# A linear-attention and two-layer kernel: every chunk handled in pairs of interleaved tokens

## The chip, the cores and the metric

The kernel runs on one core of a Trainium2 chip. The core has five engines that work side by side: TensorE (PE) for matrix products, VectorE (DVE), ScalarE (ACT), GpSimd (POOL) and SyncE (SP), which here only issues transfers. The metric is the time of one execution on the device in microseconds; lower is better. Inputs and outputs lie in the device's main memory, and 16 DMA engines move them.

## What is computed

The input is q, k and v for 4 batches, 8 heads, 768 tokens and 64 numbers a head, with a decay `lam` per head. Attention is linear, with a running state per head; its output, reshaped to 3072 tokens of 512 numbers, goes through two layers.

```python
for b in range(nb):                       # blocks of 64 tokens
    qb, kb, vb = q[:, :, sl], k[:, :, sl], v[:, :, sl]
    intra = einsum('bhic,bhjc->bhij', qb, kb) * Dmask       # causal, decayed
    intra = einsum('bhij,bhjd->bhid', intra, vb)
    inter = einsum('bhid,bhde->bhie', qb * lam_pow, kv_state)
    out[:, :, sl] = intra + inter
    kv_state = lam_block * kv_state + einsum('bhsd,bhse->bhde', kb * rev_pow, vb)
x = out.transpose(0, 2, 1, 3).reshape(3072, 512)
h = x @ w_in                              # 512 x 2048, "layer 1"
g = where(h >= 1, h, where(h <= -1, 0, (h + 1)**2 / 4))
y = g @ w_out                             # 2048 x 512, "layer 2"
```

The kernel doesn't follow the blocks of 64. It multiplies q by lam to the power of its position and k by lam to the inverse power, so that no decay is left in the products, and walks over chunks of 128 tokens with a plain causal mask and a state that is only added to.

## The kernel before

There are 24 chunks of 128 tokens, six to a batch of the input. Four chunks (512 tokens) make a stage of the two layers; there are six stages. Stage s of layer 1 needs `xT`, the transposed attention output, of its chunks; its 16 blocks of 128 hidden columns need the weights `w_in`, which come in four transfers (`W_IN`), each good for four blocks. A stage may be cut into parts by tokens (`PARTS`, L501; `FIRST`, L69, for stage 0): two parts make layer 1's matmuls 256 columns wide instead of 512, four parts 128, and a part can begin when its own chunks are there.

The work of a chunk, with the names that the profile shows:

- `f_load` (L533): SP issues the loads. q comes for two chunks at once, in runs of two tokens (512 bytes); k and v come one chunk and one token (256 bytes) a run, except for the first pair of chunks (`PF`, L65), which comes in runs of two tokens into `raw`. In such a pair a partition holds two neighbouring tokens, and "chunk" 2m + e of k and v holds the tokens of parity e of all 256.
- `cast` (L268) and `cast_q` (L275): multiply by the decay tables into bf16 `ks` and `qs`, on DVE for the first chunks, on POOL later. `cast_v` copies v on ACT.
- The transposes to `kT` and `qT`: on TensorE (`f_t`, `f_tq`) with copies by DVE and ACT for the first six chunks (`XT`), by transposing DMAs on SP's queue after them (`f_kx`, `f_qx`).
- `f_s` (L345): keys times queries, 16 matmuls on 64x64 tiles, into two PSUM banks (`ps`, `pt`; others early on). [...]
- `f_m` (L387): DVE multiplies them by the causal mask into `sc`, one bank at a time.
- `f_n` (L352): queries times the state `ub`, 8 matmuls on 64x64 tiles. `f_o` (L359): `sc` times v, 8 matmuls with all 128 rows and 64 columns. Both add up in `px`.
- `f_u` (L366): k times v, 8 matmuls of 128 rows by 64 columns, into the upper half of `px`; `f_sum` adds it to `state` on DVE, `f_ub` copies `state` to bf16 `ub` on ACT.
- `f_x` (L405): ACT copies `px` into `xT`.

The first pair has its own forms: 64x64 tiles in `f_op` (L395) and a separate `part` for the state's share, which DVE adds in `f_x`.

`px` is one tile of two PSUM banks. `pp_h` and `pp_y` hold two banks each for the layers; the first pair borrows some of them.

The order is not left to a scheduler. Every operation is registered by `add` with an engine, a duration, what it needs and a due time; `run_plan` (L202) plays this through on a small model of the engines and transfers, and issues each engine's instructions in the order that comes out, earliest due first among those ready. Each engine then works strictly in that order. `l_seq` (L509) fixes the order of the layers' pieces; `L0` (L73) that of stage 0 as (part, weight) pairs. `o_due` (L524) puts a chunk's last operation `LEAD` ahead of the layer 1 piece that needs it. `ORDER`, `GATE` and `W_AFTER` fix how the loads and the eight weight transfers on POOL's queue follow each other: a gated transfer waits until an earlier one has landed. In the later chunks (`MERGED`) the s of the next chunk and n, o, u of this one stand together as one operation of TensorE, so that its tiling mode changes less often; in the others s with n and o with u stand apart, with layer work between.

## Time and profile before

| What | Value |
|---|---|
| Median of 8 runs | 218.8 us (218.39 to 219.65) |
| The profiled execution | 218.96 us |
| Its span, first to last instruction | 217.1 us |
| First matmul of layer 1 | 18.68 us |
| Last matmul ends | 214.24 us |
| TensorE busy | 200.1 us |
| VectorE, ScalarE, GpSimd busy | 143.6, 115.5, 60.9 us |
| Packets of DMA under 512 bytes | 65810 of 87465 |

The page of the profile lists busy times, forty slices of the span, the chain of work that ended last, and the costliest groups of instructions. The timeline shows instructions in order of time: start, duration, engine, line, what is written from what, how often, and in brackets how long the engine had been idle before and who released it. [...] The profiled execution was about as long as the median run.

### The profile page before, as it was taken

To read this page: it belongs to the slowest core of one execution; us is meant where nothing else is said; L and a number is where in the kernel's file an instruction comes from. 1 tells how busy PE (TensorE), PEld (TensorE's weight loads), DVE (VectorE), ACT (ScalarE), POOL (GpSimd) and SP (SyncE) were. 2 spreads that over 40 slices of the span, in tenths; PEclk is the share of its full clock that TensorE was granted. 3 is DMA by queue.
4 is the path that set the end of the run, shared out by engine and by line. 5 is a ranking of instruction groups with operands and counts; after the bars stand their busy time and mean duration, and the time that the engine had idled before them with its cause. 6 is when DMAs were issued, how large, how long until landed. Compare 5 with 4: busy or idle time off the path is not lost.

```text
span 217.1 us, 5115 instructions
## 1 busy us (share of the span) xinstructions
PE 200.1 (92%) x2122; PEld 125.2 (58%) x2147; DVE 143.6 (66%) x233; ACT 115.5 (53%) x199; POOL 60.9 (28%) x67
## 2 busy tenths in 40 slices
PE   0579799999999999889999999999999999999994
PEld 0356687675647855657767666654444444444443
DVE  3394786889743992797899996857876364554301
ACT  3454677364617664676565846746645544455030
POOL 5590094065633413833506325100000000000000
PEclk9999999999999999999999999999999999999999
DMA  5999999999998999999999999991101001110122
GB/s 165 278 215 206 249 179 219 226 213 213 172 203 182 223 168 221 175 231 209 235 186 204 174 282 179 271 284 39 48 3 48 23 25 48 51 48 0 48 100 97
DMA packets 87465, 34.42 MB, mean 159 GB/s; under 512 B 65810, under 2 KB 84498, under 8 KB 87442
## 3 DMA queue, kind: packets, MB, share of 16 engines
q1 hardware_dynamic: 83216, 29.89, 66.8%
q0 software_dynamic: 4224, 4.19, 11.7%
q8 instruction: 17, 0.28, 0.6%
q14 instruction: 6, 0.05, 0.1%
q10 hardware_dynamic: 2, 0.00, 0.0%
HBM read 27.26 MB, written 6.29 MB: 155 GB/s over the span
## 4 chain that ended last, share of the span: by engine, by line
PE 53%; issue 1%; DVE 0%
PE py L474 24%; PE ph L426 23%; PE px L363 2%; PE ps L349 2%; PE py L468 1%; PE px L370 1%; PE px L356 1%; PE ph L468 0%; PE pt L349 0%; DVE osb L486 0%
## 5 line engine op out<-in xcount | busy, mean ns | idle before, releaser
L426 PE MATMUL ph<-xT,w_in_sb 128*128 128x256 bf16 (+2 forms) x764 | 95.8, 274 | 3.4 <-ACT xT L415 2.6
L435 ACT ACTIVATE r<-ph,one 128x512 bf16<-128x512 f32 x96 | 65.6, 688 | 48.4 <-PE ph L426 36.9
L474 PE MATMUL py<-w_out_sb,gT 128*128 128x512 bf16 x347 | 85.6, 379 | 1.8 <-issue 1.1
L426 PEld LDWEIGHTS <-w_in_sb 128*128 128x128 bf16 x768 | 64.1, 98 | 28.0 <-issue 3.6
L474 PEld LDWEIGHTS <-gT 128*128 128x128 bf16 x368 | 34.7, 98 | 36.9
L445 DVE TENSOR_SCALAR t<-r 128x1024 bf16<-128x1024 bf16 x48 | 25.6, 533 | 22.3 <-ACT r L435 22.3
L456 DVE TENSOR_TENSOR gT<-w,t 128x1024 bf16<-128x1024 bf16 x48 | 39.1, 815 | 1.5
L451 DVE TENSOR_TENSOR w<-r,t 128x1024 bf16<-128x1024 bf16 x48 | 36.2, 753 | 1.4
L281 POOL TENSOR_TENSOR qs<-x0f,tab_q 128x512 bf16<-128x512 f32 x23 | 27.2, 1202 | 26.5 <-DMA x0f<-in_q_dram 19.4
L273 POOL TENSOR_TENSOR ks<-x1f,tab_k 128x512 bf16<-128x512 f32 x20 | 23.6, 1188 | 35.8 <-issue 15.6
L479 ACT COPY osb<-py 128x512 f32<-128x512 f32 x23 | 13.4, 585 | 22.3 <-PE py L474 21.2
L393 DVE TENSOR_TENSOR sc<-ps,causal 128x512 bf16<-128x512 f32 x22 | 15.1, 687 | 13.4 <-PE pt L349 13.1
L415 ACT CAST xT<-px 128x512 bf16<-128x512 f32 x22 | 12.9, 585 | 13.6 <-PE px L370 8.3
L393 DVE TENSOR_TENSOR sc<-pt,causal 128x512 bf16<-128x512 f32 x21 | 14.3, 681 | 0.0
L295 ACT CAST v<-x2f 128x512 bf16<-128x512 f32 x22 | 13.6, 618 | 0.2 <-DMA x2f<-in_v_dram 0.2
L377 DVE TENSOR_TENSOR state<-state,px 128x256 f32<-128x256 f32 x16 | 6.7, 419 | 8.2 <-ACT xT L415 4.7
L349 PEld LDWEIGHTS <-kT 64*64 64x64 bf16 x384 | 6.6, 112 | 6.9 <-issue 4.6
L385 ACT CAST ub<-state 128x256 bf16<-128x256 f32 x20 | 8.0, 402 | 4.6 <-DVE state L375 2.5
L349 PE MATMUL ps<-qT,kT 64*64 64x128 bf16 x184 | 10.0, 230 | 0.5 <-DVE kT L314 0.5
L363 PE MATMUL px<-sc,v 128*64 128x128 bf16 x176 | 9.1, 225 | 0.0
L349 PE MATMUL pt<-qT,kT 64*64 64x128 bf16 x168 | 8.7, 222 | 0.0
L363 PEld LDWEIGHTS <-v 128*64 128x64 bf16 x176 | 5.6, 109 | 4.3 <-issue 2.5
(62 smaller groups left out, 77.9 us busy)
## 6 DMA issues: line engine op xcount, KB each, us to landing
x0f<-in_q_dram SPq DMA_DIRECT2D x12, 512.0 KB, 5.5
out_dram<-osb SPq DMA_DIRECT2D x23, 256.0 KB, 2.6
x1f<-in_k_dram SPq DMA_DIRECT2D x22, 256.0 KB, 5.1
x2f<-in_v_dram SPq DMA_DIRECT2D x22, 256.0 KB, 5.4
w_in_sb<-in_moe_w_in_dram POOLq DMA_DIRECT2D x4, 512.0 KB, 8.2
w_out_sb<-in_moe_w_out_dram POOLq DMA_DIRECT2D x4, 512.0 KB, 8.0
raw<-in_k_dram SPq DMA_DIRECT2D x1, 512.0 KB, 5.5
raw<-in_v_dram SPq DMA_DIRECT2D x1, 512.0 KB, 6.7
```

The source lines that it names most:

```text
L273: eng.tensor_tensor(ho(ks[c]), hs(qkv_ld[c, 1]), ho(_bc(tab, 2, D)), op=AX.mult)
L281: eng.tensor_tensor(ho(qs[m, e]), hs(qkv_ld[m, 0][:, :, e]), ho(_bc(tab_q[:, e, m % (NCB // 2), :], 2, D)), op=AX.mult)
L295: nc.scalar.copy(out=v_sb[c % NV], in_=qkv_ld[c, 2])
L349: nc.tensor.matmul(pst[c, r][HD[i], b, :], lhsT=kT[c][HD[r], b, HD[i]], rhs=q_cols(2 * (c // 2) + i if c // 2 in PF else c, b, HD[r]), sta ...
L363: nc.tensor.matmul(px[HD[g], j, :128], lhsT=v_sb[c % NV][:, 2 * j + g, :], rhs=sc_sb[c][:, r, b, :], start=(c % NCB == 0 and j % 2 == 0), ...
L393: nc.vector.tensor_tensor(sc_sb[c][:, g], pst[c, g], _bc(causal, 1, HP), op=AX.mult)
L426: nc.tensor.matmul(ph[:, j * m:(j + 1) * m], lhsT=w_in_sb[:, ko, (ni + j) * 128:(ni + j + 1) * 128], rhs=xT[s][:, ko, tok], start=(ko == 0 ...
L435: nc.scalar.activation(out=o, in_=x, func=AF.Relu, bias=one[:, 0:1])
L445: nc.vector.tensor_scalar(t, r, 0.5, 1.0, op0=AX.mult, op1=AX.min)
L451: nc.vector.tensor_tensor(w, r, t, op=AX.subtract)
L456: nc.vector.tensor_tensor(gT[s][:, f - RW * n:f, tok].rearrange("p (a b) m -> p a b m", a=RW), w.rearrange("p a (b m) -> p a b m", m=m), t ...
L474: nc.tensor.matmul(py_t[s, ms], lhsT=gT[s][:, ko, ms * 128:(ms + 1) * 128], rhs=w_out_sb[:, ko, :], start=(ko == 0), stop=(ko == FO - 1))
```

## The change

All chunks now go through the paired form; the single-chunk form is gone.

- k and v are loaded for two chunks at a time in runs of two tokens, like q. The keys, queries, state and output products of a pair are three operations of TensorE: A (`f_n` first phase, `f_s` of parity 0), B (`f_s` of parity 1 with `f_n`'s second phase inside), C (`f_c`, both parities, both chunks). `f_c` and `f_u` run on 64x64 tiles: 32 matmuls each for a pair.
- `px` has two banks, one for each chunk of the pair, and `f_n` works in two phases, so that the two row halves of the array write to different banks at a time. `f_u` writes to banks of its own instead of `px`. A third pair of a batch computes only the state of its first chunk.
- For the first pair the state's product is `f_n0`, with a state `ubz` padded with zeros.
- `warm` issues matmuls with no use for the result, in the gaps that the plan shows on TensorE before its own time 18000 ns: as many as fill 0.8 of each gap at 107 ns.
- Some early casts are split between DVE and POOL (`SHARED`), kT of chunk 1 is copied by ACT, x of chunk 1 too.
- The orders and due times differ: stage 0 takes all four weights for its first part and then for the second; stage 1 has two parts instead of four, stage 3 one instead of two; `LEAD` is 6000 instead of 4500; the loads' gates are new. From pair 5 on (`MERGED`) u of the next pair stands behind C.

```diff
-    LD = 6
+    LD = 3
...
     RW, NR = 2, 3
-    XT, NQT, NQK, RING = 6, 4, 4, 3
+    XT = 6
+    NQT, NQK, RING = 4, 4, 3
     W_IN = (4, 4, 4, 4)
-    MERGED = tuple(range(12, 24))
-    LATE = (3,)
+    MERGED = tuple(range(5,12))
     SWITCH = 96
     W_OF = [i for i, n in enumerate(W_IN) for _ in range(n)]
-    ORDER = [0, 1, 2, 3, (0, 0), (0, 1), (0, 2), (0, 3), 4, (1, 0), (1, 1), 5, (1, 2), (1, 3)]
-    PF = (0,)
-    D0 = (8350, 11900, 15450, 19000)
+    ORDER = [0, 1, (0, 0), (0, 1), (0, 2), (0, 3), 2, (1, 0), (1, 1), 3, (1, 2), (1, 3)]
+    D0 = (8350, 10000, 15450, 17000)
     FIRST = [(0, 2), (2, 4)]
-    L0 = [(0, 0), (0, 1), (1, 0), (1, 1), (0, 2), (1, 2), (0, 3), (1, 3)]
-    GATE = {(0, 0): ("lq", 1), 4: 1, 6: 5}
-    LORD = {0: (0, 1, 2), 2: (0, 1, 2)}
+    L0 = [(0, 0), (0, 1), (0, 2), (0, 3), (1, 0), (1, 1), (1, 2), (1, 3)]
+    GATE = {(0, 0): ('lq', 1), 2: 0, (1, 0): 2, 3: 4, (1, 2): 4}
...
-    px = pp_o.tile([128, HP, 256], F32)
+    px = pp_o.tile([128, 2, HP, 128], F32)
...
     MMS, FETCH = {"s": 16, "u": 8}, 1300
-    FIRST_BYTE = 2350
-    LDD, QXD, KXD, STD = 20000, 7000, 7000, 3000
-    ON_POOL, ON_DVE = (1,), ((0, 1),)
-    W_AFTER = {1: ("cq", 1, 1)}
+    FIRST_BYTE = 2750
+    LDD, STD = 16000, 3000
+    QXD, KXD = 7000, 7000
+    AD, BD = (8000, 4000), (4000, 2000)
+    UD, TD = (9000, 9000), (8000, 8000)
+    KT_ACT = (1,)
+    K_DVE = (0,1,2,3,5)
+    ON_DVE = ((0,0),(0,1),(2,1))
+    SHARED = (1,(0,1))
+    W_AFTER = {1: ("cq", 1, 0)}
...
+        pe_end = WARM[0]
         for t, _, x in sorted(out_seq, key=lambda p: p[:2]):
+            if x.eng == "PE" and pe_end is not None:
+                n = int((t - pe_end - 50) * WARM[3] / WARM[2])
+                if t > WARM[1]:
+                    pe_end = None
+                else:
+                    pe_end = t + x.ns
+                    if DBG and n > 0:
+                        print(f"{t / 1e3:9.3f} 0 WARM {n} {x.key}")
+                    warm(max(n, 0))
+                    if x.key in (("s", 1), ("C", 0)):
+                        hot[0] = None
...
+    WARM = (2700, 18000, 107, 0.8)
+    hot = [None]
+
+    def warm(n):
+
+        for _ in range(n):
+            if hot[0] is None:
+                hot[0] = pp_h.tile([128, MS], F32, name="ph", tag="ph")
+            nc.tensor.matmul(hot[0][:, :256], lhsT=ident, rhs=_bc(ident, 1, 2), start=True, stop=True)
...
+    TILES = [(0, 0), (1, 1), (0, 1), (1, 0)]
+    pu = {}
+
+    def f_s(a, inter=None):
+
+        m = a // 2
+        pools = (((pp_s, "ps"), (pp_h, "ph")), ((pp_h, "ph"), (pp_y, "py")))[a] if m == 0 else ((pp_s, "ps"), (pp_t, "pt"))
         for r, (pl, nm) in enumerate(pools):
...
-    TILES = [(0, 0), (1, 1), (0, 1), (1, 0)]
-
-    def f_s(c):
-        new_s(c)
+            pst[a, r] = pl.tile([128, HP, 128], F32, name=nm, tag=nm)
         for b in range(HP):
             for r, i in TILES:
-                nc.tensor.matmul(pst[c, r][HD[i], b, :], lhsT=kT[c][HD[r], b, HD[i]],
-                                 rhs=q_cols(2 * (c // 2) + i if c // 2 in PF else c, b, HD[r]), start=True, stop=True)
-
-    def f_n(c):
+                nc.tensor.matmul(pst[a, r][HD[i], b, :], lhsT=kT[a][HD[r], b, HD[i]], rhs=q_cols(2 * m + i, b, HD[r]),
+                                 start=True, stop=True)
+            if b == 0 and inter is not None:
+                f_n(m, inter)
+
+    def f_n(m, phase):
+
         for n in range(2):
             for r, g in TILES:
-                h = 4 * r + g + 2 * n
-                nc.tensor.matmul(px[HD[g], h // 2, :128], lhsT=ub[(c - 1) % NUB][HD[r], h % 4, :], rhs=q_cols(c, h % 4, HD[r]),
-                                 start=(n == 0), stop=True, skip_group_check=True)
-
-    def f_o(c):
+                i = r ^ phase
+                c, h = 2 * m + i, 4 * r + g + 2 * n
+                if c % NCB:
+                    nc.tensor.matmul(px[HD[g], i, h // 2, :], lhsT=ub[(c - 1) % NUB][HD[r], h % 4, :], rhs=q_cols(c, h % 4, HD[r]),
+                                     start=(phase == 0 and n == 0), stop=True, skip_group_check=True)
...
+    def f_n0():
+
         for j in range(HP):
             for g in range(2):
                 r, b, _ = place(2 * j + g)
-                nc.tensor.matmul(px[HD[g], j, :128], lhsT=v_sb[c % NV][:, 2 * j + g, :], rhs=sc_sb[c][:, r, b, :],
-                                 start=(c % NCB == 0 and j % 2 == 0), stop=True, skip_group_check=True)
-
...
+                nc.tensor.matmul(px[HD[g], 1, j, :], lhsT=ubz[:, b, r, :], rhs=q_cols(1, b),
+                                 start=(j == 0), stop=True, skip_group_check=True)
+
+    def f_c(m):
...
+        for e in (1, 0):
+            for j in range(HP):
+                for i, g in TILES:
+                    c, (r, b, _) = 2 * m + i, place(2 * j + g)
+                    nc.tensor.matmul(px[HD[g], i, j, :], lhsT=v_sb[(2 * m + e) % NV][HD[i], 2 * j + g, :],
+                                     rhs=sc_sb[2 * m + e][HD[i], r, b, :],
+                                     start=(c % NCB == 0 and e == 1 and j == 0), stop=True, skip_group_check=True)
+
+    def f_u(m):
+        both = m % (NCB // 2) < NCB // 2 - 1
+        for i in range(2 if both else 1):
+            pl, nm = (((pp_y, "py"), (pp_t, "pt")), ((pp_s, "ps"), (pp_y, "py")), ((pp_s, "ps"), (pp_t, "pt")))[min(m, 2)][i]
+            pu[i] = pl.tile([128, HP, D], F32, name=nm, tag=nm)
+        for e in range(2):
             for b in range(HP):
-                for r in range(2):
-                    nc.tensor.matmul(px[HD[r], b, 128:128 + D], lhsT=ks[a][rows, 2 * b + r, :], rhs=v_sb[a % NV][rows, 4 * r + b, :],
-                                     start=(n == 0 and b % 2 == 0), stop=True, skip_group_check=True)
+                for i, r in TILES:
+                    if i == 0 or both:
+                        nc.tensor.matmul(pu[i][HD[r], b, :], lhsT=ks[2 * m + e][HD[i], 2 * b + r, :],
+                                         rhs=v_sb[(2 * m + e) % NV][HD[i], 4 * r + b, :],
+                                         start=(e == 0 and b == 0), stop=True, skip_group_check=True)
 
     def f_sum(c):
         if c % NCB == 0:
-            nc.vector.tensor_copy(state, px[:, :, 128:128 + D])
+            nc.vector.tensor_copy(state, pu[c % 2])
         else:
-            nc.vector.tensor_tensor(state, state, px[:, :, 128:128 + D], op=AX.add)
```

The due times, the loads and the new operations:

```diff
-    T0, STEP = 22000, 1057
-    LEAD, APART = 4500, 3000
-    PARTS = {1: 4, 2: 2, 3: 2, 4: 1}
+    T0, STEP = 22000, 1075
+    LEAD, APART = 6000, 3000
+    PARTS = {1: 2, 2: 2, 4: 1}
+    EARLY = 3
...
+            t = ld.tile([128, H, 2, D], F32, name=f"x{x}f", tag=f"x{x}f")
             i = (k, v)[x - 1][b, :, s0:s0 + 2 * C, :].rearrange("h (j e) d -> j h (e d)", e=2)
             d = nc.sync.dma_start(out=t.rearrange("p h e d -> p h (e d)"), in_=i)
             for e in range(2):
                 qkv_ld[c + e, x] = t[:, :, e]
-        else:
-            t = ld.tile([128, H, D], F32, name=f"x{x}f", tag=f"x{x}f")
-            d = nc.sync.dma_start(out=t, in_=(k, v)[x - 1][b, :, s0:s0 + C, :].rearrange("h p d -> p h d"))
-            qkv_ld[c, x] = t
-        ld_dma[("ld", c, x) if x else ("lq", c // 2)] = d.ins.name
...
+        for c in (c0, c0 + 1):
+            e = "DVE" if c in K_DVE else "POOL"
+            both = c in SHARED
+            if both:
+                add(("cast", c, 9), "POOL", 800, lambda c=c: cast(c, nc.gpsimd, slice(2, 4)), [("lk", m), ("cast", c, 1)])
+            add(("cast", c, 1), e, 380 if both else 690 if e == "DVE" else 1060,
+                lambda c=c, eng=(nc.vector if e == "DVE" else nc.gpsimd), bs=slice(0, 2 if both else 4): cast(c, eng, bs),
+                [("lk", m), ("cast", c - 1, 1), ("t", c - NQK), u_op(m - NQK // 2)])
+            add(("cast", c, 2), "ACT", 640, lambda c=c: cast_v(c), [("lv", m), ("C", m - NV // 2), u_op(m - NV // 2), ("cast", c - 1, 2)])
+        for i in range(2):
...
+        u_need = lambda m: [x for c in (2 * m, 2 * m + 1) for x in (("cast", c, 9), ("cast", c, 1), ("cast", c, 2))] + \
+            [("sum", 2 * m - 1 if m % (NCB // 2) else 2 * m - 2), ("m", 2 * m - 1, 0), ("m", 2 * m - 1, 1), ("kT", 2 * m + 1) if m != 1 else None]
+        if m not in MERGED:
+            MMS["u", m] = 32
+            add(("u", m), "PE", 240 + 2 * SWITCH, lambda m=m: f_u(m), u_need(m), due=od - UD[m == 1], extra=FILL)
...
+        if m == 0:
+            for a in range(2):
+                MMS["s", a] = 16
+                add(("s", a), "PE", 416, lambda a=a: f_s(a), qk(a) + [("m", a - 1, 0)], due=od - 2500 + 500 * a, extra=FILL)
+                mask(a, ("s", a))
+            MMS["B", 0], MMS["C", 0] = 8, 32
+            add(("B", 0), "PE", 412, f_n0, [("ub", 0)] + qk(1), due=od - 1500, extra=FILL)
+            add(("C", 0), "PE", 640, lambda: f_c(0), [("B", 0), ("m", 0, 1), ("m", 1, 0), ("m", 1, 1), ("cast", 1, 2)], due=od, extra=FILL)
         else:
...
+            old = [("x", c0 - 2), ("x", c0 - 1)]
+            MMS["A", m] = MMS["B", m] = 24
+            add(("A", m), "PE", 336 + 2 * SWITCH, lambda m=m: (f_n(m, 0), f_s(2 * m)),
+                qk(c0) + sums + old + [("m", c0 - 1, 0), ("m", c0 - 1, 1), ("ub", c0 - 1), ("ub", c0), ("kT", c0 + 1), ("C", m - 1)],
+                due=od - AD[m == 1], extra=FILL)
+            mask(c0, ("A", m))
+            add(("B", m), "PE", 336 + 2 * SWITCH, lambda m=m: f_s(2 * m + 1, 1),
+                qk(c0 + 1) + [("A", m), ("m", c0, 0), ("m", c0, 1)], due=od - BD[m == 1], extra=FILL)
+            mask(c0 + 1, ("B", m))
+            nxt = m + 1 in MERGED and m + 1 < NPB
+            MMS["C", m] = 64 if nxt else 32
+            add(("C", m), "PE", 448 + 240 * nxt + 2 * SWITCH, lambda m=m, nxt=nxt: (f_c(m), f_u(m + 1) if nxt else None),
+                [("B", m), ("m", c0 + 1, 0), ("m", c0 + 1, 1), ("cast", c0 + 1, 2)] + (u_need(m + 1) if nxt else []), due=od, extra=FILL)
+        for c in (c0, c0 + 1):
+            add(("x", c), "ACT", 600, lambda c=c: f_x(c),
+                [("C", m), ("x", c - 1), ("x", c - 2), ("l1", (c // CPS - 2) * FO - 1)])
```

## The prediction, made before the changed kernel ran

> **What bounds the kernel now.** Four views, in this order: the page's slices, the chain that ended last, the timeline of TensorE, the table of windows.
>
> ```profile
> span 217.1 us, 5115 instructions
> ...
> PE   0579799999999999889999999999999999999994
> ...
> DMA  5999999999998999999999999991101001110122
> ```
>
> Each of the forty digits is a slice of 5.43 us. PE is full from the fourth slice on; the DMA engines are full until slice 27, about 145 us, and idle after it. The chain:
>
> ```profile
> 97.75 0.04 issue
> 97.79 1.91 PE ph L426 x16
> ...
> 214.24 0.02 issue
> 214.26 0.29 DVE osb L486
> ```
>
> From 97.79 us to the last matmul at 214.24 us the chain never leaves TensorE. What is saved of TensorE's work or of its waits is saved in the end time. The waits stand in its timeline:
>
> ```profile
> 6.78 0.61 PE L307 MATMUL py<-ident,qs 128*128 128x128 bf16 x4 [3.13 <-POOL qs L281]
> ...
> 18.68 2.88 PE L426 MATMUL ph<-xT,w_in_sb 128*128 128x256 bf16 x16 [0.42 <-DVE xT L413]
> ...
> 23.16 1.80 PE L426 MATMUL ph<-xT,w_in_sb 128*128 128x256 bf16 x15 [0.57 <-ACT xT L415]
> ...
> 26.34 0.93 PE L426 MATMUL ph<-xT,w_in_sb 128*128 128x256 bf16 x7 [0.68 <-ACT xT L415]
> ```
> ```profile
> 85.17 1.91 PE L426 MATMUL ph<-xT,w_in_sb 128*128 128x256 bf16 x16
> ...
> 87.48 1.92 PE L426 MATMUL ph<-xT,w_in_sb 128*128 128x256 bf16 x16
> ...
> 91.52 0.93 PE L426 MATMUL ph<-xT,w_in_sb 128*128 128x256 bf16 x7 [0.56 <-ACT xT L415]
> ...
> 97.79 1.91 PE L426 MATMUL ph<-xT,w_in_sb 128*128 128x256 bf16 x16 [0.82 <-ACT xT L415]
> ```
>
> Layer 1 begins at 18.68 us, and its first sixteen matmuls take 2.88 us where sixteen of the same form take 1.75 us in the chain at 105.79 us. Four times TensorE stands still for xT, 0.56 to 0.82 us each. Last, the transfers:
>
> ```profile
> 5.00:10.80 5.80, 2.83 (x36) 2.04 (x38) 2.26 (x4) 2.21 (x4) 3.09 (x2) 1.00 1.20 280
> 10.80:18.60 7.80, 6.20 (x128) 4.43 (x128) 6.52 (x13) 4.22 (x8) 5.21 (x6) 1.00 1.31 213
> 40.00:140.00 100.00, 96.94 (x1237) 67.27 (x1252) 78.70 (x120) 58.99 (x104) 42.14 (x36) 1.00 1.11 208
> ```
>
> The last two numbers are the DMA share and GB/s. Both shares are full, but with the loads in runs of two tokens (5 to 10.8 us) 280 GB/s move, and 208 where k and v come token by token.
>
> **An account of before.** Layer 1 is 256 matmuls of 128 columns at 0.0556 us (32 start within 42.75 to 44.53), 384 of 256 at 0.1094 (16 in 1.75) and 128 of 512 at 0.2156 (4 in 0.86): 14.2 + 42.0 + 27.6 = 83.8. Layer 2 is 384 x 0.2156 = 82.8. Attention: the matmuls at 85.17 fill their places until 86.92 and the next begin at 87.48, so s with n adds 0.56; by the same sum o with u adds 0.57 before 89.80; a merged chunk (s, n, o, u) adds 1.03 between 108.40 and 109.43. Over the pieces that fall after 18.68, the shorter first and last chunks of a batch included, I get 22.6. Four groups of transposes at 0.22: 0.9. Sum 190.1, of 214.24 - 18.68 = 195.6. Some 5.5 us are waits and the slow start: 1.0 slow clock, 2.6 the four waits, the rest small. Matmul records that are missing were counted as done.
>
> [...] 0.213 us a matmul after 18.8, 0.109 from 20.74 on. [...] the four of a round at 21.96 start within 0.01, and rounds follow every 0.055. [...] Here s with n is six rounds, 0.32, and adds 0.56: 0.24 for going in and out. [...]
>
> **The change part by part.**
>
> *State and output products.* Before, o is 8 matmuls of 128 rows by 64 columns a chunk (four rounds of two, 0.25 from 108.79 to 109.04) and u 8 (0.12). After, f_c is 32 tiles of 64x64 a pair, eight rounds of 0.054 = 0.43, and f_u 32 of 64 columns, eight rounds at 0.03 = 0.24. So C with u is 0.67 + 0.2 of switches = 0.87, A and B are six rounds and two switches each, 0.56. A merged pair: 1.98 against 2 x 1.03; an unmerged pair (m 1 to 4; u on its own, 0.44): 2.18 against 2 x 1.13. Eleven pairs: 8.9 + 13.6 - 0.2 for chunks without n = 22.3, against 22.6. The last pair of a batch pays a full u for one chunk; that is in it. No trace shows 32 tiles of 64 columns at the fast clock. Bounds for it: [...] above, the 0.0134 a matmul that s shows (16 in 0.214), 0.43. I take 0.24, as u's 0.03 a round shows it; [...]
>
> *Parts.* Stage 1 goes from four parts to two (128 matmuls of 256 columns for 256 of 128: 14.23 - 14.00), stage 3 from two to one (14.00 - 13.80): -0.4.
>
> *Loads.* Ten pairs' k and v, 10.5 MB, go from 208 towards 280 GB/s: 13 us of DMA time. None of it is on the path; PE hides it. What it can do is let POOL's casts begin earlier (they waited 19.4 us for q), and with LEAD from 4500 to 6000 make the copies of xT come before layer 1 asks. I take the waits at 91.52 and 97.79 as gone, 1.4, and 0.5 as coming back as waits between A, B and C.
>
> *The start.* q lands at 5.1 as before. DVE makes the first half, DVE and POOL share the second. Ahead of the first transpose stand about (5.8 - 2.7) x 0.8 / 0.107 = 23 filling matmuls: [...] all slow, 8.5. Before, the transposes began at 6.78. After that TensorE is at full clock: a group of transposes takes 0.39 (at 32.75) for 0.61. Then copies, s(0), s(1) to 12.1, four masks at 0.60 on DVE to 13.5, the sum, two copies of ub, B, C to 15.6, two copies of x at 0.58: 16.8, and up to 18.5 if the casts of chunks 2 and 3 (0.69 to 1.55 each) get between on DVE. Queued behind the filling matmuls is all of attention; if they run long, this is what slips.
>
> The weights decide as well. w_in 0 is issued when the second q has landed, 10.80, as before, and lands at about 17.4 (shortest landing 6.6). The next q is gated on the second weight before and issued at 21.03; the last w_in lands at 26.7 (15.3 + 11.4). After, the same bytes in fewer runs, but pair 2's loads are let in after weight 0. Estimate: 17.4, 20.3, 23.5, 26.8. The order of stage 0 now takes all four weights for part 0 first, 1.75 us each: it ends at 26.8 + 1.75 = 28.6. Between 17.4 and 28.6 there are 7.0 of layer 1 and 3.5 of pair 1's attention and transposes: I take 1.5 of waits instead of the 1.25 at 23.16 and 26.34. Slow clock: 0 instead of 1.0.
>
> *Small edits.* One table less, one mask less, f_part gone, x(1) on ACT instead of DVE, kT(1) on ACT: DVE and ACT had 2 us of slack there; nothing. More instructions (some 350 matmuls and as many loads): [...] +0.1, in the rest.
>
> *Sum.* Start 17.4 + layers 166.6 - 0.4 + attention 22.3 + transposes 1.3 (six groups fall after the start) + waits 1.5 in stage 0 and 2.3 elsewhere (5.5 - 1.0 - 1.25 - 1.4 + 0.5, rounded down) = 211.0. To the end of the span another 2.9 as before: 213.9. The profiled run took 218.96 for a span of 217.1, so +1.86: 215.8. That run lies 0.16 above the median of 218.8: I say 215.6.
>
> **Rivals.** (1) *Stage 0 waits for weights.* If pair 2's loads share the engines with weights 1 to 3, each lands 3.5 apart, the last at 28, and TensorE has too little to fill with: start and clock are lost again, 217.7. For it: DMA is full there. Against: before had the same bytes. (2) *Small tiles are bound by issue*: +2.2, 217.8. Against it is u's 0.03. (3) *The chain of a pair becomes the bound, slower.* Each pair is a chain A, two masks, B, two masks, C with u, two sums, two ub, on an in-order TensorE: about 7 us by its rows. If the hand-written due times put one of its parts on PE before its mask is done, layer matmuls behind it stand still too. Place: PE's A, B and C. Price: one wait of the size seen at 97.79 a pair, 0.6, over eleven pairs, +6.6: 222. It decides from 3.2 / 11 = 0.3 us a pair. For it: DVE is busy 79 of 100 us from 40 to 140, and `t` there swings from 0.42 to 1.26. Against: 12 us a pair are at hand. (4) *More than I count*: TensorE starts at 17 and all waits but 2 us go: 213.2. That the products don't run on 64x64 tiles is excluded by the operands' slices.
>
> **Chances.** Forecast 0.52, own range 214 to 217.2; (1) 0.15; (2) 0.08; (3) 0.18; (4) 0.07. Faster by over 0.2% (0.44 us, about what a measurement can tell from no change): 0.73; within: 0.06; slower: 0.21. The range leaves out the far end of (3) and the best of (4): 212.8 to 219.8.
>
> **What would show it.** Right: layer 1's first matmul near 17.4 at 0.109 a matmul; A, B near 0.56 and C with u near 0.87 on PE; no wait over 0.5 for xT after 40 us; DMA idle some 10 us sooner. Wrong: filling matmuls that end after 8.5; waits of layer 1 for w_in between 19 and 28; PE's idle between 40 and 140 above the 3.1 of before.

## The result and the profile after

The changed kernel takes 220.32 us (median of 20 runs, 219.04 to 221.63), the kernel before 218.52 in the same comparison (57 runs, 217.75 to 220.46). The ratio is 1.0075, with a 95% interval of 1.0057 to 1.0093: slower by 1.8 us. The forecast was 215.6. The profiled execution of the changed kernel took 221.5 us for a span of 219.8; it lies 1.2 us above the median, so the sums below are made against its own 219.8.

The page's head, its slices (now of 5.5 us each) and its count of packets:

```profile
span 219.8 us, 5487 instructions
...
PE   3999878999979999999999999999999999999994
...
DMA  5999999999999999999999936311011001110122
...
DMA packets 64586, 34.43 MB, mean 157 GB/s; under 512 B 20402, under 2 KB 61618, under 8 KB 64562
```

TensorE is full from the second slice instead of the fourth: those are the filling matmuls. It then has gaps in slices 5 to 7 and 12, from 22 to 38 us and about 63 us; before had that of slice 5 and shallow ones in slices 17 and 18, which are gone. The DMA engines are full until slice 23 instead of 27 (126 and 147 us), and 20402 packets instead of 65810 are under 512 bytes: the loads did what they were to do. The chain of waits no longer begins in the middle of the run, at 97.75:

```profile
14.40 13.22 DMA w_in_sb<-in_moe_w_in_dram
27.67 1.06 PE ph L439 x8
29.88 3.67 PE ph L439 x31
...
62.65 1.41 DVE gT L469
64.06 1.21 DVE sc L421 x2
66.00 1.67 PE py L487 x7
```

It goes back through the last transfer of `w_in`, on whose landing TensorE goes on at 27.67, to the first loads, and passes through VectorE from 44 to 65 us, and again from 90 to 97, before it stays on TensorE. The same places in TensorE's timeline (start, duration, then in brackets how long it had stood idle and who released it):

```profile
4.16 5.09 PE L274 MATMUL ph<-ident 128*128 128x256 bf16 x23
9.04 0.71 PE L329 MATMUL py<-ident,qs 128*128 128x128 bf16 x8
...
23.83 2.52 PE L439 MATMUL ph<-xT,w_in_sb 128*128 128x256 bf16 x21
26.28 0.64 PE L388 MATMUL px<-sc,v 64*64 64x128 bf16 x32
27.67 1.16 PE L439 MATMUL ph<-xT,w_in_sb 128*128 128x256 bf16 x9 [0.75 <-DMA w_in_sb<-in_moe_w_in_dram]
29.88 3.66 PE L439 MATMUL ph<-xT,w_in_sb 128*128 128x256 bf16 x31 [1.05 <-ACT xT L428]
```

The last of the 23 filling matmuls gives way to the transposes at 9.04 us, and layer 1 begins at 19.75 us (18.68 before). The gap at 29.88 is odd: it stops layer 1 after nine matmuls, one past a whole unit of eight (two blocks of hidden columns, four matmuls each). The table of windows, the stretch from 25 to 40 us, before and then after (span of the window, then busy time and count of each engine, clock, DMA share, GB/s):

```profile
25.00:40.00 15.00, 14.07 (x161) 11.46 (x159) 11.53 (x18) 10.50 (x17) 7.77 (x8) 1.00 1.16 212
```
```profile
25.00:40.00 15.00, 12.31 (x152) 10.25 (x151) 10.45 (x19) 10.34 (x19) 4.85 (x6) 1.00 1.14 232
```

TensorE is busy 1.8 us less in these 15, which is the size of the whole loss. One can also count the layers' weight loads (their records are complete: all 976 or 1168) with the columns of their matmuls, in units of 2400 columns. The trace's 512-column matmuls start 0.216 us apart (a record of one lasts 0.379 us on average, so neighbours overlap, and starts are what to count by), and at that pace a unit takes 1.01 us. So one sees how many of the layers' 163.8 units are done:

| done by | before | after | before with fillers (e2) | the same, xT by part (e11) | after, xT by part, new gates (e16) |
|---|---|---|---|---|---|
| 30 us | 6.9 | 6.4 | 8.0 | 8.7 | 8.2 |
| 50 us | 23.7 | 20.9 | 24.3 | 25.2 | 21.3 |
| 70 us | 41.0 | 36.9 | 41.4 | 42.5 | 39.1 |
| 100 us | 63.1 | 60.5 | 64.1 | 65.0 | 62.3 |
| 200 us | 150.4 | 148.1 | 151.3 | 152.3 | 151.7 |

The changed kernel is 0.5 units behind at 30 us, 2.8 at 50, 4.1 at 70, and 2.3 at 200; part of the difference in the middle may be attention that it does earlier. So most of the loss arises in stages 0 and 1 and is kept. The experiments ask what holds TensorE there.

### The profile page after: what moved, and what is told of

The parts are those of the page before. It is cut to its first block, busy times and chain, and to the rows that moved or that the text cites. A ratio compares the mean times of both kernels' runs of the same rounds, so it can differ in the third digit from the quotient of the medians.

```text
span 219.8 us, 5487 instructions
## 1 busy us (share of the span) xinstructions
PE 205.3 (93%) x2317; PEld 121.4 (55%) x2343; DVE 149.2 (68%) x235; ACT 115.1 (52%) x200; POOL 60.0 (27%) x63
## 2 busy tenths in 40 slices
DMA packets 64586, 34.43 MB, mean 157 GB/s; under 512 B 20402, under 2 KB 61618, under 8 KB 64562
## 4 chain that ended last, share of the span: by engine, by line
PE 70%; DVE 12%; DMA 9%; issue 2%; POOL 2%; ACT 1%; SPq 1%; ACTq 0%
PE ph L439 31%; PE py L487 31%; DMA w_in_sb<-in_moe_w_in_dram 6%; DVE gT L469 4%; DVE w L464 4%; DMA x0f<-in_q_dram 3%; PE ps L360 2%; DVE t L458 2%; PE px L388 2%; DVE sc L421 2%; PE px L372 1%; PE py L481 1%; POOL w_in_sb L163 1%; SPq L557 1%; PE ps L401 1%
## 5 line engine op out<-in xcount | busy, mean ns | idle before, releaser
L439 PE MATMUL ph<-xT,w_in_sb 128*128 128x256 bf16 (+1 forms) x573 | 95.5, 308 | 2.5 <-ACT xT L428 1.1
L487 PE MATMUL py<-w_out_sb,gT 128*128 128x512 bf16 x345 | 87.0, 379 | 2.3 <-issue 1.6
L439 PEld LDWEIGHTS <-w_in_sb 128*128 128x128 bf16 x576 | 54.9, 98 | 32.6 <-issue 2.1
L469 DVE TENSOR_TENSOR gT<-w,t 128x1024 bf16<-128x1024 bf16 x48 | 40.5, 845 | 1.3
L464 DVE TENSOR_TENSOR w<-r,t 128x1024 bf16<-128x1024 bf16 x48 | 39.9, 832 | 1.3
L300 POOL TENSOR_TENSOR qs<-x0f,tab_q 128x512 bf16<-128x512 f32 (+1 forms) x22 | 26.1, 1203 | 43.2 <-DMA x0f<-in_q_dram 32.0
L292 POOL TENSOR_TENSOR ks<-x1f,tab_p 128x512 bf16<-128x512 f32 (+1 forms) x20 | 25.1, 1274 | 16.5 <-PE pt L401 8.8
L274 PE MATMUL ph<-ident 128*128 128x256 bf16 x68 | 11.2, 322 | 0.0
L409 DVE TENSOR_TENSOR state<-state,ps 128x256 f32<-128x256 f32 x8 | 3.4, 419 | 8.2 <-PE pt L401 6.9
L274 PEld LDWEIGHTS <-ident 128*128 128x128 bf16 x68 | 7.4, 115 | 2.1 <-issue 0.4
```

Source lines behind the costliest of these rows:

```text
L274: nc.tensor.matmul(hot[0][:, :256], lhsT=ident, rhs=_bc(ident, 1, 2), start=True, stop=True)
L292: eng.tensor_tensor(ho(ks[c])[:, bs], hs(qkv_ld[c, 1])[:, bs], ho(_bc(tab, 2, D))[:, bs], op=AX.mult)
L300: eng.tensor_tensor(ho(qs[m, e])[:, bs], hs(qkv_ld[m, 0][:, :, e])[:, bs], ho(_bc(tab_q[:, e, m % (NCB // 2), :], 2, D))[:, bs], op=AX.mult)
L439: nc.tensor.matmul(ph[:, j * m:(j + 1) * m], lhsT=w_in_sb[:, ko, (ni + j) * 128:(ni + j + 1) * 128], rhs=xT[s][:, ko, tok], start=(ko == 0 ...
L464: nc.vector.tensor_tensor(w, r, t, op=AX.subtract)
L469: nc.vector.tensor_tensor(gT[s][:, f - RW * n:f, tok].rearrange("p (a b) m -> p a b m", a=RW), w.rearrange("p a (b m) -> p a b m", m=m), t ...
```

## The experiments

Each kernel is compared with the kernel before on the same chip; the ratio is to that.

### The filling matmuls

*e1*, the changed kernel without them:

```diff
-                    warm(max(n, 0))
+                    warm(0)
```

> The changed kernel without the filling matmuls. Theory start: the 23 fillers ahead of the first transposes all ran slow (0.213 each, 4.16 to 9.04) and held attention back 3 us; without them the first transposes begin near 6.2, layer 1 near 17.5 to 18, but at the slow clock (+1.0): about 1 us under the changed kernel, 219.3. Rival: the start is set by weights and by ScalarE's copies, and what fillers cost they give back in clock: 220.3 within 0.4. Second rival: the slow clock reaches further into the start than before and it gets slower, 221.

Measured: 221.78 us, ratio 1.0141 (1.0118 to 1.0164): 1.5 us slower than the kernel after. *e2*, the kernel before with the fillers and nothing else of the change (the lines on `WARM`, `hot` and `warm` of the diff above):

> The kernel before with the fillers of the change alone. Theory start: the transposes slip from 6.78 to about 9, the slow clock of layer 1 (1.0) goes; sum about +0.5 to +1: 219.3. Rival: the slip is covered by the wait for weight 0 and the clock is a net gain: 217.6.

Measured: 217.89 us, ratio 0.9957 (0.9939 to 0.9976), faster than both kernels. Timelines of TensorE, of e1 and then of e2:

```profile
17.21 1.87 PE L439 MATMUL ph<-xT,w_in_sb 128*128 128x256 bf16 x8
19.80 2.27 PE L439 MATMUL ph<-xT,w_in_sb 128*128 128x256 bf16 x16
```
```profile
3.59 4.23 PE L276 MATMUL ph<-ident 128*128 128x256 bf16 x22
```

Without fillers layer 1 begins 2.5 us sooner, but its first eight matmuls take 1.87 us instead of 1.04: it starts at half the pace. With fillers it starts late and fast, and fast wins. In e2 22 fillers take 4.23 us, since the pace doubles at 7.0. What the traces show of a slow clock at the start is this pace, 0.213 us from one matmul of 256 columns to the next where it is 0.109 later, and that the record of the granted clock begins, at full, where the pace doubles: at 9.24 us in the kernel after, at 20.71 in the kernel before. So this part gains about what the prediction gave it, and all the rest of the change costs some 3 us (221.78 against 218.7).

*e5* and *f9* ask whether the late start of 19.75 is the loss: at most nine fillers in a gap (in e5 only ahead of 12 us of the plan, in f9 everywhere).

```diff
-                    warm(max(n, 0))
+                    warm(min(max(n, 0), 9))
```

> The changed kernel with at most 9 fillers in a gap, and none after 12 us of the plan. Theory start: the first transposes near 6.2 and the clock fast before layer 1: 218.8, better than without any. Rival (weights bound stage 0, first part at all four weights): under 0.4 from the changed kernel, because layer 1 then waits for weight 3 at 27.67 all the same.

> The changed kernel with at most 9 fillers in each gap, all gaps up to 18 us of the plan kept. Theory start: transposes near 6.2 and fast clock at layer 1 (the clock stays fast, where it fell back from 13.9 to 20.7 with fillers cut off at 12): layer 1 at about 17.5, when weight 0 lands, 219.3; TensorE is then stopped by weight 3 near 27 as before. Rival: nothing beyond 219.96, since weights and not the clock set stage 0: 219.7 to 220.3.

Measured: e5 219.96 us, 1.0067 (1.0043 to 1.0090); f9 220.64, 1.0090 (1.0062 to 1.0117). Layer 1 begins at 17.52 and 17.67, two us sooner, and neither kernel can be told apart from the kernel after. In f9 TensorE waits for every `w_in` in turn, 0.46 us for the third and 1.27 for the last. An earlier start is worth nothing here while the weights land when they do.

### The orders

*e3*: stage 0 in the order of before. *e4*: the parts of before.

```diff
-    L0 = [(0, 0), (0, 1), (0, 2), (0, 3), (1, 0), (1, 1), (1, 2), (1, 3)]
+    L0 = [(0, 0), (0, 1), (1, 0), (1, 1), (0, 2), (1, 2), (0, 3), (1, 3)]
```
```diff
-    PARTS = {1: 2, 2: 2, 4: 1}
+    PARTS = {1: 4, 2: 2, 3: 2, 4: 1}
```

> The changed kernel with the order of stage 0 of before (two weights for both parts, then the others). Theory weights: the wait for weight 3 (0.75 at 27.67) goes, but part 1 is asked for after two weights, and pair 1 is done only at 27, so TensorE waits there instead: no gain, 220 to 222. Rival: the planner moves pair 1 up and a gain of 0.8 to 1.5 shows, 219.

> The changed kernel with the parts of before (stage 1 in four parts, stage 3 in two). If the parts do what the prediction priced, it is 0.4 us slower than the kernel after: 220.7. If the larger parts cost waits for xT, it is faster than after by 0.3 to 1: 219.3 to 220.0, and the layer work done by 60 us rises from 29.2 us towards 30.5.

Measured: 220.86 us, 1.0092 (1.0059 to 1.0126), and 220.25, 1.0090 (1.0055 to 1.0126). Neither moves the time by itself. The order of stage 0 was not tried again together with the later edits; the parts were (e17).

*e6*, *e7*, *e8*: f9 with other gates of the transfers.

```diff
-    GATE = {(0, 0): ('lq', 1), 2: 0, (1, 0): 2, 3: 4, (1, 2): 4}
+    GATE = {(0, 0): ('lq', 1), 2: 3, (1, 0): 2, 3: 4, (1, 2): 4}           # e6
+    GATE = {(0, 0): ('lq', 1), 2: 0, (1, 0): ('lv', 2), 3: 4, (1, 2): 4}   # e7
+    GATE = {(0, 0): ('lq', 1), 2: 2, (1, 0): ('lv', 2), 3: 4, (1, 2): 4}   # e8
```

> f9 with pair 2's loads let in after weight 3 instead of weight 0. Theory contention: weight 3 lands near 25 instead of 27, and the two waits behind it (about 0.9 for the weight, 1.2 for xT) shrink to under 0.5 together; but pair 2 comes 2 to 4 us later, and the wait at pair 2's transposes and u grows: total within 1 us of f9. Rival, weights are late for another reason: the landing of weight 3 doesn't move by more than 0.5.

> f9 with the first w_out transfer let in after pair 2's v has landed, instead of after weight 2. Theory contention: v of pair 2 lands some 4 us sooner (cast of v near 32 instead of 36.9) and the wait of about 1.2 at pair 2's u on TensorE goes: about -1 against f9, 218.3. Rival: layer 2 then waits for w_out and the gain is lost: as f9 or slower.

> f9 with pair 2's loads after weight 2 and w_out after pair 2's v. Theory contention: both waits shrink, 217.8, near the kernel before with fillers (217.89). Rival, pairs are too coarse for the start (twice the bytes before the first token of pair 2 can be used): still at least 1 us above 217.89.

Measured: 225.58 us, 1.0305 (1.0253 to 1.0357); 220.76, 1.0109 (1.0068 to 1.0149); 221.67, 1.0126 (1.0080 to 1.0172). All three missed what was hoped for. With pair 2 held back (e6) the weights are early, no wait for them is over 0.1 us, and pair 2 is late instead: TensorE's gaps between 40 and 44.1 us sum to 2.6. That is half of the 4.9 us that e6 is slower than f9. Later waits for masks and `xT` follow (1.5 us at 65.8, 0.7 at 68.3), and behind those the clock is at half from 66.6 to 73.4 us (from 60 to 80 us the granted clock is 0.83 on average). All six runs of e6 have lost clock: its mean over a run, with 1 for full speed, is 0.985 to 0.991, where the kernel before has 0.998 or more. One wait stood through all of these runs, early weights or not: 1.05 us for `xT` behind C of pair 1.

### A wait that nothing needs

ScalarE's timeline of the kernel after:

```profile
26.38 0.69 ACT L448 ACTIVATE r<-ph,one 128x512 bf16<-128x512 f32 x1 [0.25 <-PE ph L439]
28.75 1.07 ACT L428 CAST xT<-px 128x512 bf16<-128x512 f32 x2 [1.68 <-PE ph L439]
29.71 0.70 ACT L448 ACTIVATE r<-ph,one 128x512 bf16<-128x512 f32 x1
...
36.94 1.14 ACT L315 CAST v<-x2f 128x512 bf16<-128x512 f32 x2 [1.09 <-DMA x2f<-in_v_dram]
```

C of pair 1 begins on TensorE at 26.28 and takes 0.67; the two copies of `px` into `xT` begin only at 28.75, and what released them is a matmul of layer 1. That is the unit of part 0 which itself had waited for the weights until 27.67. It reads other columns of the tile than the copies write. And the next unit of part 0 waits for these copies after one matmul. `xT` is `[128, KO, MS]`: the columns of a part lie in each of the four blocks `ko`. The first matmul of a unit reads block 0, below everything that the copies write; from block 1 on its columns lie between columns that the copies write, and the span from the first to the last column overlaps. That the waits come from dependencies taken by such spans was the author's guess, and no trace shows how they are taken; what can be tried is whether the waits go with the layout. So lay the tile out part by part (*e10*; *e11* is e2 with the same edit):

```diff
+        n = MS // len(parts[sx])
+        xs = xT[sx].rearrange("p h m -> p (h m)").rearrange("p (a h m) -> p a h m", h=KO, m=n)
-        o = xT[sx][:, :, off:off + C].rearrange("p h (j e) -> p h j e", e=2)
+        o = xs[:, off // n, :, off % n:off % n + C].rearrange("p h (j e) -> p h j e", e=2)
...
+        xs = xT[s].rearrange("p h m -> p (h m)").rearrange("p (a h m) -> p a h m", h=KO, m=m)[:, tok.start // m]
...
-                                 rhs=xT[s][:, ko, tok], start=(ko == 0), stop=(ko == KO - 1))
+                                 rhs=xs[:, ko], start=(ko == 0), stop=(ko == KO - 1))
```

> The changed kernel with stage 0's to 4's xT laid out part by part (for each part its four blocks of columns side by side, the same 2048 columns in all), so that what the copies of a later part write and what the matmuls of an earlier part read no longer lie between each other. Theory (false waits): in the kernel after, the copies of chunks 2 and 3 stand on ACT until 28.75 us although the products were there at 26.9, because they wait for the matmuls of part 0 that read other columns of the same tile and these wait for the last w_in; then the second matmul of the next unit of part 0 waits 1.05 until 29.88 for these copies. With the layout by part the copies follow the products at about 27.1 and the wait of 1.05 is gone: about -1.0, 219.3 us, and layer 1 goes on at 28.66. Rival 1 (true waits): the units need the copies, the wait stays at about 1 us, 220.3. Rival 2 (the loads of pair 2 set the time from here): the wait at 29.9 goes but comes back as longer waits for pair 2 between 33 and 45 us: 220.0 to 220.4.

> The kernel before with the filling matmuls and with xT laid out part by part; nothing else of the change. In the run of before with the filling matmuls alone (217.9 us), waits of 0.74 at 21.4 and 0.73 at 89.7 stop layer 1 after one matmul of a unit, 0.68 at 25.30 after the merged chunk. Theory (false waits): these go, about -1.5 to -2: 216.2 us, which would beat both kernels. Rival (true waits, or the weights take their place): 217.9; the wait moves to w_in.

Measured: e10 220.69 us, 1.0068 (1.0042 to 1.0095); e11 216.58, 0.9911 (0.9882 to 0.9939). Lines of e10, TensorE and then ScalarE:

```profile
26.71 4.77 PE L442 MATMUL ph<-xT,w_in_sb 128*128 128x256 bf16 x40 [0.49 <-DMA w_in_sb<-in_moe_w_in_dram]
...
34.74 0.61 PE L322 MATMUL pt<-ident,ks 128*128 128x128 bf16 x8
37.65 0.31 PE L401 MATMUL ps<-v,ks 64*64 64x64 bf16 x8 [2.30 <-ACT v L315]
...
38.76 3.36 PE L442 MATMUL ph<-xT,w_in_sb 128*128 128x256 bf16 x16 [0.28 <-ACT r L451]
```
```profile
26.28 1.07 ACT L430 CAST xT<-px 128x512 bf16<-128x512 f32 x2
...
36.99 1.14 ACT L315 CAST v<-x2f 128x512 bf16<-128x512 f32 x2 [3.20 <-DMA x2f<-in_v_dram]
```

The theory on the wait holds: the copies begin at 26.28, and from 26.71 forty matmuls follow without a stop. The median doesn't follow: v of pair 2 is cast at 36.99 as it was at 36.94, and TensorE, which arrives sooner, starts no matmul from 35.13 to 37.65 (in the kernel after from 37.19 to 37.61). This is the second rival: what was taken ahead of a late transfer is given back at it.

This profiled run gives back more than it took. It took 222.1 us, 1.4 above its median, and behind the stop sixteen matmuls take 3.36 us instead of 1.91: the clock is at half from 38.4 to 41.8 us. Such 3.4 us at half are 1.7 us, or 0.8% of the mean clock of a run. Nine of e10's twenty runs have a mean clock of 0.990 to 0.992, and their median is 222.1 us; the eleven others, at 0.997 or more, have 219.5, near the 219.3 that the theory expected. (The kernel after has one such run among 21, before none.) This split was made afterwards, and 219.5 is not clear of the noise of the kernel after. Which stop took the clock in the runs that were not profiled is not known.

In the kernel before, where k and v come by single chunks, the same edit keeps its gain. Around the wait of e2, and then e11:

```profile
21.26 0.28 PE L446 MATMUL ph<-xT,w_in_sb 128*128 128x256 bf16 x1
22.12 1.80 PE L446 MATMUL ph<-xT,w_in_sb 128*128 128x256 bf16 x15 [0.57 <-ACT xT L435]
```
```profile
21.14 1.92 PE L449 MATMUL ph<-xT,w_in_sb 128*128 128x256 bf16 x16
...
24.45 6.58 PE L449 MATMUL ph<-xT,w_in_sb 128*128 128x256 bf16 x56 [0.68 <-ACT xT L437]
...
90.91 1.91 PE L449 MATMUL ph<-xT,w_in_sb 128*128 128x256 bf16 x16 [0.28 <-ACT r L458]
...
95.70 1.91 PE L449 MATMUL ph<-xT,w_in_sb 128*128 128x256 bf16 x16 [0.82 <-ACT xT L437]
```

The 0.74 after one matmul at 21.4 us is gone, and the 0.73 at 89.7. At 24.45 and 95.70 layer 1 waits at the head of a unit whose copies really are not there, and at 90.91 some 0.5 us of wait for `ub` and `r` have come in place of the other. e11 is 1.3 us faster than e2 by the medians, 1.0 by the ratios, and no kernel of the study is faster.

### Both at once

*e12*: f9 with xT by part and the gate of e7. *e16*: pair 3's loads after the last `w_in` as well. *e14*: f9 with xT by part, w_out 0 after pair 2's k.

```diff
-    GATE = {(0, 0): ('lq', 1), 2: 0, (1, 0): 2, 3: 4, (1, 2): 4}
+    GATE = {(0, 0): ('lq', 1), 2: 0, (1, 0): ('lv', 2), 3: 4, (1, 2): 4}   # e12
+    GATE = {(0, 0): ('lq', 1), 2: 0, (1, 0): ('lv', 2), 3: 3, (1, 2): 4}   # e16
+    GATE = {(0, 0): ('lq', 1), 2: 0, (1, 0): ('lk', 2), 3: 4, (1, 2): 4}   # e14
```

> The changed kernel with at most nine filling matmuls a gap, xT laid out by part, and w_out 0 issued after pair 2's v has landed. With xT by part alone (220.7 us) the copies of chunks 2 and 3 came at 26.28 and the wait at 29.9 went, but 3.1 us of wait stood before pair 2's state product, whose v was cast at 36.99. Theory (the loads of pair 2 bound the stretch from 25 to 45 us, the false waits lie ahead of them): with v early both are gone, layer work done by 50 us rises from 20.4 towards 22.5, and the kernel takes 218.0 us or less. Rival (whatever is taken here is lost behind: masks, parts and copies of pairs 3 and 4): 219.8 to 220.7.

> As the run before it in this list, with pair 3's loads let in after the last w_in instead of after w_out 0. In the run with w_out 0 held for pair 2's v the DMA engines were all but idle (0 to 30 GB/s) from about 30 to 33 us. Theory: that hole fills, pair 3 comes some 3 us sooner, and waits after 45 us shrink: -0.3 to -1.0 against the run before it. Rival: pair 3's bytes then share the engines with pair 2's v, and the wait at 35 to 38 us returns: 0 to +1.5.

> As the first of these (nine filling matmuls a gap at most, xT by part), but w_out 0 is issued when pair 2's k has landed, not its v: w_out 0 and v share the engines. Theory: no hole in the transfers, v some 2 us later than with w_out held for it: between the two, 218.5 to 219.5.

Measured: e12 220.01 us, 1.0074 (1.0046 to 1.0102); e16 218.89, 1.0009 (0.9988 to 1.0030); e14 219.86, 1.0049 (1.0029 to 1.0069), which is not told apart from e12 and missed its 218.5 to 219.5. e12 missed: v is cast at 34.07, the wait before the state product is gone, and the time is taken by the next transfer. First TensorE of e12, then one window of e12 and the same of e16:

```profile
45.96 0.38 PE L490 MATMUL py<-w_out_sb,gT 128*128 128x512 bf16 x1 [1.79 <-DMA w_out_sb<-in_moe_w_out_dram]
```
```profile
30.00:33.00 3.00, 2.96 (x29) 2.42 (x27) 2.97 (x5) 2.42 (x4) 2.14 (x3) 1.00 0.05 9
```
```profile
30.00:33.00 3.00, 2.80 (x28) 2.28 (x26) 2.97 (x5) 2.52 (x5) 2.11 (x3) 1.00 1.08 273
```

In e12 the DMA engines move 9 GB/s for three us, because everything behind is gated on v; in e16 it is 273, and the wait is gone. e12's runs fall into two groups. Ten have a mean clock of 0.999 or more and take 218.8 to 220.2 us, median 219.5: 0.9 less than f9's runs of 0.997 or more. Eight have 0.992 and take 221.1 to 222.6. So there is a gain, and the runs that lose the clock lose more than it. The trace of e12 is of the first group; of e16's fourteen runs two are of the second.

Against f9 (1.0062 to 1.0117) the interval of e16 (0.9988 to 1.0030) is clear: 1.7 us are gained by the layout of xT and the order of the transfers together, where by the medians the layout alone (e10) and the gate on v alone (e7) gained nothing; the gate of pair 3 alone wasn't tried. That is the loss of the change in size, to 0.1 us, and not in cause: the kernel before gains by the layout as well, and with the fillers and the layout it takes 216.6. TensorE in e16:

```profile
17.60 1.04 PE L442 MATMUL ph<-xT,w_in_sb 128*128 128x256 bf16 x8
...
23.39 1.92 PE L442 MATMUL ph<-xT,w_in_sb 128*128 128x256 bf16 x16 [0.99 <-DMA w_in_sb<-in_moe_w_in_dram]
...
26.83 4.76 PE L442 MATMUL ph<-xT,w_in_sb 128*128 128x256 bf16 x40 [0.95 <-DMA w_in_sb<-in_moe_w_in_dram]
...
39.26 0.30 PE L372 MATMUL px<-qT,ub 64*64 64x128 bf16 x7 [1.12 <-ACT ub L416]
```

Layer 1 begins 0.9 us sooner than in e11 (17.60 against 18.48) and then waits about 1 us for each of the last two weights and 1.1 for the state of pair 2. The two traces place what is left of the loss, though their runs are only 1.15 us apart (217.89 and 216.74), where the medians are 2.3: from the first matmul of layer 1 to 40 us TensorE's gaps sum to 3.4 us against 0.9 in e11, from 40 to 140 us to 0.24 against 1.25. So it lies ahead of 40 us, in waits for transfers and for what is made of them. Why the change leaves it was not settled. That a pair's k and v are half a megabyte each before its first chunk can be used, where a single chunk needs a quarter, is the likely reason, but only argued.

### Parts and LEAD

The prediction priced the larger parts at -0.4 us and put the end of two waits to LEAD. *e13*: e11 with the change's PARTS and LEAD. *e15*: with its PARTS alone. *e18*: with its LEAD alone. *e17*: e16 with the parts of before.

```diff
-    PARTS = {1: 4, 2: 2, 3: 2, 4: 1}
+    PARTS = {1: 2, 2: 2, 4: 1}      # e13, e15; e17 the other way
...
-    LEAD, APART = 4500, 3000
+    LEAD, APART = 6000, 3000        # e13, e18
```

> As the run before it in this list (before, filling matmuls, xT by part), with the change's PARTS (stage 1 in two parts, stage 3 whole) and LEAD of 6000. The prediction priced the parts at -0.4 of matmul time. Theory: -0.2 to -0.4 against that run, some 215.9. Rival: fewer parts make the first unit of a stage need more of xT, and the waits for xT grow by as much or more: +0.3 to +1.

> The kernel before with the filling matmuls, xT by part and the change's PARTS (stage 1 in two parts, stage 3 whole), with LEAD left at 4500. With LEAD 6000 as well the time was 222.2 against 216.6 without both. If PARTS is the cause: 221 to 223. If LEAD is: about 216.3, 0.3 below for the cheaper matmuls that the prediction counted.

> The kernel before with filling matmuls and xT by part (216.6 us), and LEAD 6000 for 4500. The prediction held that this makes the copies of xT come before layer 1 asks, and took away the waits at 91.5 and 97.8; in the run with LEAD 4500 they stand at 90.9 (0.71) and 95.7 (0.85). If that is right: about -1.4, 215.2. Rival: attention is placed sooner than its loads, and its own waits stop the layer matmuls behind it: 216.6 to 218.

> The changed kernel with all the edits that helped it (nine filling matmuls a gap at most, xT by part, w_out 0 after pair 2's v, pair 3's loads after the last w_in: 218.9 us) and with the parts of before (stage 1 in four, stage 3 in two). In the kernel before with filling matmuls and xT by part the larger parts cost 4.1 us. If they cost as much here, about 215 us, the best of all. If a pair brings two chunks at once, so that a part of one chunk is no finer than what attention delivers, nothing but the 0.4 of dearer matmuls: 219.3.

Measured: e13 222.23 us, 1.0180 (1.0132 to 1.0227); e15 220.67, 1.0112 (1.0068 to 1.0155); e18 216.89, 0.9887 (0.9854 to 0.9921); e17 220.60, 1.0080 (1.0060 to 1.0100). LEAD alone does nothing that can be told: in e18 the wait at 95.7 is gone and that at 90.9 has grown from 0.7 to 1.1 with TensorE waiting for `ub`. The larger parts cost the kernel before 4.1 us. In the changed kernel they cost nothing (e4), and with all other edits going back to the parts of before even costs 1.7 (e17); my expectation of 215 for e17 was wrong. So parts are not the cause of the loss here, and their price belongs to the plan around them. TensorE of e15, and two of its windows:

```profile
111.03 4.48 PE L497 MATMUL py<-w_out_sb,gT 128*128 128x512 bf16 x20
117.58 0.28 PE L376 MATMUL px<-qT,ub 64*64 64x128 bf16 x8
...
118.26 3.10 PE L497 MATMUL py<-w_out_sb,gT 128*128 128x512 bf16 x8
```
```profile
115.50:118.20 2.70, 0.88 (x41) 0.78 (x40) 0.47 (x2) 1.10 (x2) 0.42 (x1) 1.00 0.80 166
...
120.00:122.00 2.00, 2.00 (x6) 0.62 (x5) 0.00 (x0) 0.00 (x0) 1.27 (x2) 0.50 1.37 236
```

A merged chunk comes some 2 us too late, because the transfer that makes its transposed keys lands late; behind it the clock falls to 0.50, and eight matmuls take 3.10 us instead of 1.90. The price is not the clock, though: this is the only one of e15's six runs with a mean clock as low as 0.992, and the five others take 219.9 to 223.2 us. It is waits: TensorE's gaps from the first matmul of layer 1 on sum to 6.0 us against 2.5 in e11, with 1.8 for these keys, 1.1 for masks at 62 us and the rest in small ones.

## Why the prediction was wrong, step by step

Its sum had the last matmul end at 211.0; in the profiled run it ends at 216.5. The terms, predicted and measured: start of layer 1 17.4 and 19.75; attention 22.3 and 22.8; transposes 1.3 and 0.9; layers 166.2 as counted; waits, which is what then is left, 3.8 and 6.9; behind the last matmul 2.9 and 3.3. The waits, +3.1, are the step that failed: "I take 1.5 of waits" in stage 0, which are 3.2, and 2.3 elsewhere, which are 3.7. The start, +2.35, was wrong too, but f9 shows that it is worth nothing by itself. Of the signs of being wrong that were named, two came plainly (fillers that end after 8.5, a wait for w_in at 27.67) and the third narrowly: TensorE is idle for 3.35 us from 40 to 140, for 3.06 before.

- **The start.** The sum let only a part of the fillers run at the slow pace, an estimate that no trace of before shows, and named 8.5 for the case that all do (23 at 0.213 from 3.65 us). They began at 4.16, and all 23 ran at 0.213, 4.9 us. After C two casts of v (1.13 us) stood ahead of the copies of x on ScalarE, which the prediction had only suspected on VectorE. The copies end at 18.75, and five more fillers, from 19.20 on, stand directly ahead of layer 1. Yet f9 starts at 17.67 and is no faster, and w_in 0, 1 and 2 landed about when estimated (f9 begins on them at 17.67, 20.2 and 23.1; estimate 17.4, 20.3, 23.5). A start can't be worth more than the weights behind it allow.
- **Waits in stage 0, 1.5.** They are about 3.2: 1.1 at 27.67 for the last w_in (0.75 in the timeline, the rest behind C), 1.05 to 1.2 at 29.88 and 1.0 for pair 2 between 36.8 and 38.7. The first is the wait that the first rival named, to the number: the weights land 3.5 to 3.7 us apart, the last at 27.6 for its 28. Its 217.7 and its lost clock did not come with it. The second is the false wait on xT. Before had it too: the 0.57 that the prediction quotes at 23.16, after one matmul of a unit, is the same thing, as e2 and e11 show, and was read there as a true wait for a copy. That this wait stops layer 1 one matmul into a unit was not asked about. The third is the transfers of pair 2.
- **Waits elsewhere, 2.3, with two "gone".** They are 3.7. The two waits for xT at 91.5 and 97.8 are gone, and no other for xT stands after 40 us; but in their place TensorE waits about 0.5 for ScalarE's `r` at 95.9 and 0.4 for the state at 97.3. e18 shows the same of LEAD by itself: the wait for xT goes, and one for `ub` grows. The third rival, a pair's chain on an in-order TensorE, has one clear case: B of pair 3 is placed between 63.6 and 66.0, and the layer work behind it waits about 1.4 for the masks, 0.72 and 0.39 of it as gaps. These three make 2.3; the rest is in no single place. On VectorE and on POOL there:

```profile
59.90 1.27 DVE L458 TENSOR_SCALAR t<-r 128x1024 bf16<-128x1024 bf16 x1
61.20 1.41 DVE L464 TENSOR_TENSOR w<-r,t 128x1024 bf16<-128x1024 bf16 x1
62.65 1.41 DVE L469 TENSOR_TENSOR gT<-w,t 128x1024 bf16<-128x1024 bf16 x1
63.99 0.68 DVE L421 TENSOR_TENSOR sc<-ps,causal 128x512 bf16<-128x512 f32 x1
```
```profile
59.67 2.40 POOL L300 TENSOR_TENSOR qs<-x0f,tab_q 128x512 bf16<-128x512 f32 x2 [4.22 <-issue]
62.03 2.93 POOL L292 TENSOR_TENSOR ks<-x1f,tab_p 128x512 bf16<-128x512 f32 x2
```

  While POOL casts, w and gT take 1.41 us each, where 0.68 and 0.69 stand just ahead, and the masks come 2 us late. The wait differs from run to run (none in e5 and e7, 1.2 in e10, 2.2 in e1). In this trace the twelve w and gT that run beside such casts for nine tenths of their time or more take 1.13 to 1.42 us, and the seventy that run beside none at most 0.69; why is not shown. A wait of this size for the masks happens once, not once a pair, so rival 3 with its 222 is not what came.
- **Attention.** A and B measure 0.555 for 0.56, C 0.667 for 0.63, C with u 0.92 for 0.87, u 0.47 for 0.44. Rival 2, with u's small tiles at 0.0134 us each and 0.43 for 32, did not come, and the products save nothing and cost little: +0.5 against the sum, +0.2 against before. (By the prediction's own prices its 8.9 and 13.6 are 4 x 2.18 = 8.7 and 7 x 1.98 = 13.9, 0.1 more.) The 0.03 a round taken from u before holds for 32 tiles: those of u at 13.13 us start in rounds of four, the four within 0.01, and most rounds follow after 0.03.
- **Parts.** The 0.4 of matmul time is there; that parts have another price, in waits, was not looked for. In the changed kernel it is nothing, in the kernel before 4.1 us.
- **Loads.** The DMA engines are full for some 20 us less, but from 40 to 126 us, while they are full in both kernels, 232 GB/s move for 203 before, not the 280 that the sum went towards. None of it was thought to lie on the path. One part of it does: pair 2's v, whose issue begins at 18.0, is cast as it lands at 36.9 and holds TensorE there (e10; in e12 and e16 it comes sooner and the wait is gone). The prediction looked at the total of the bytes and not at the one transfer that is needed first.
- **Fillers.** Right in kind and about in size: 1.5 us in the changed kernel (e1), 0.8 in the kernel before (e2), for the 1.0 of slow clock that the sum took away.
- **Small edits.** The +0.1 for more instructions leaned on pauses of 0.05 us between matmuls. They are places where one matmul's record is missing: two steps of 0.216 less one record of 0.379 leave 0.053. Where all records are there, as in e10, e11 and e16, none is left.

## What to carry to other kernels

Where a wait stops an instruction in the middle of a unit whose inputs were all there, look at how the tile is laid out before looking at the clock: a layout with one stretch for each part can end it, and here it was worth 1.0 to 1.3 us in a kernel that was already tuned. A gain ahead of a late transfer makes the stop at that transfer longer, and in about half of the runs of e10 and e12 the clock was lost as well: move both, and look at the clock of every run, before calling either worthless. And a plan written out by hand prices its parts as a set; the same change of one constant cost 4.1 us in one plan and nothing in another. The best kernel found is the kernel before with the fillers and with xT by part, 216.58 us, 0.9911 of before (0.9882 to 0.9939); LEAD 6000 makes no difference that can be told on top.
